# A Fourier mixing block turned over: transposed output, folds on both axes, groups of 384 tokens, the second weight matrix loaded later

## The chip, the cores and the metric

The kernel runs on one core of one Trainium2 chip. The metric is device time in microseconds (us) of one execution; lower is better. The profile names the engines PE (TensorE matmul), PEld (its weight loads), DVE (VectorE), ACT (ScalarE), POOL (GpSimd) and SP (the queue that issues most loads).

## The reference

Two blocks follow each other: attention restricted to equal hash buckets, then a Fourier mixing block with a normalised two-layer network. There are 4 batches, 8 heads, 768 tokens, 64 columns per head, 512 model columns and 2048 hidden ones.

```
q_bits = (q @ proj > 0); k_bits = (k @ proj > 0)       # 6 bits: the bucket
scores = where(q_bucket == k_bucket, q @ k.T / 8, -1e9)
x = softmax(scores) @ v                                # (B, S, H*D) = (4, 768, 512)
mixed = real(fft(fft(x, axis=1), axis=2))              # along tokens, then columns
u = x + mixed
un = (u - mean(u)) / sqrt(var(u) + 1e-6)               # over the 512 columns
out = u + maximum(un @ w_ch1, 0) @ w_ch2
```

The weights arrive as 64-bit floats and all matmuls on the path below run in f32.

## The kernel before, in words

The program is traced in an order written out by hand, and a planner then gives each engine its fixed queue: of the instructions that are ready and whose buffers are free it takes the one that was traced first. Every tile tag has a fixed number of buffers; a tile waits until an earlier one of its tag has had its last use. The main loop (L867) runs attention of batch 0 to 3. Attention is a generator that yields after each half step; at each yield the loop draws steps from a second generator, `other`: in batch 0 one step of `weights`, in batches 1 to 3 two steps of `mix` of the batch before. What is left of `other` at the end of a batch is traced there; the mix of batch 3 comes last, alone.

*Attention* treats heads in pairs, n = 0 to 15. `prepare` (L600) transposes q and k of the pair, makes hash bits on PE and buckets `qb`, `kb`. Then for each half g of the queries (384 each) and each of 6 key tiles c comes a half step, 48 per batch: `weigh` (L660) runs two `sc` matmuls, one per head, on 64 rows of the array each, then `exp` on ACT and two masked products on DVE (L675) into one of three `pk` buffers; DVE adds `pk` to the running sum `acc` (L745); `values` (L681) of the half step before runs two `oo` matmuls, one per head, on 64 columns of the array each. At the last c, `finish` (L694) sums on PE (L702), goes through a chain on DVE (L710 to L721: transpose, reciprocal, broadcast, transpose, product) and transposes the result `xn` back to tokens by columns (L726). `oo` has one of two `ps_o` banks per half.

*Mix* (L759) makes sums and differences of the two token halves (`pm`) and of mirrored columns (`eo`), then `y`, the token transform, on PE (L795, 30 matmuls with 193 columns), mirrors `y` (L804), and for each of three groups of 256 tokens: two times `z`, the column transform (L815, 512 columns), u = x + z, mean and variance, `un`, four transposes (`ut`); 16 times `h` (L841: 4 matmuls with 256 columns, then relu on ACT and DVE in turn); two times `o` (L856, 16 matmuls with 512 columns), u + o and the store (L862). There are 66 mix steps per batch, so at two per half step they are used up after 33 of 48.

*Weights* (L583) load the two weight matrices in 32 pieces. `narrow` (L547) turns each from 64-bit to 32-bit: a load from POOL's queue into `st`, nine DVE instructions on 512 columns, one POOL addition (L581). Its buffer is one of the two of tag `fft`, which the mix uses too.

PSUM has eight banks: two tiles of two banks for `sc` (`ps_sc`), two for `oo` (`ps_o`), two for everything else (`ps_1`, by `pt`, L483). Only the last mix, when `attending` is off, takes tiles of all three in turn. `evac` (L494) copies by DVE and ACT in turn.

Of the kernel before, what the change touches and what calls it, by code (L numbers as in the profile page):

```python
# [10 lines left out]
F32 = mybir.dt.float32  # L11
BF16 = mybir.dt.bfloat16
# [35 lines left out]
def _consts():  # L48
# [24 lines left out]
    for r in range(P):  # L73
        h, bit = divmod(r % 32, NBITS)
        if h < 2:
            pw[r, h] = 2.0**bit
    return {
        "pw": np.ascontiguousarray(pw, dtype=np.float32),
        "seq": np.ascontiguousarray(seq, dtype=np.float32),
# [370 lines left out]
def _main(  # L450
# [73 lines left out]
    pwf = wt([P, 2, P], F32, "fft", "pwf")  # L524
# [10 lines left out]
    NPK = 3  # L535
# [5 lines left out]
    seq = const.tile([P, 2, NT // 2, 2 * NK], F32, tag="seq", name="seq")  # L541
    chan = const.tile([P, NDC, DM], F32, tag="chan", name="chan")
# [3 lines left out]

    def narrow(dst, src, name):  # L547


        st = wt([P, 5 * WC], F32, "fft", name)  # L550
# [32 lines left out]
    def weights():  # L583
        nc.sync.dma_start(seq, cn["seq"].ap())
        nc.sync.dma_start(chan, cn["chan"].ap())
        for wsb, wdr in ((w1, moe_w_ch1), (w2, moe_w_ch2)):
            for c in range(wdr.shape[0] // P):
                for f in range(0, wdr.shape[1], WC):
                    dst = wsb[:, c, f : f + WC]
                    src = wdr[c * P : (c + 1) * P, f : f + WC]  # L590
                    if wdr.dtype == I64:
                        narrow(dst, src, f"st{wdr.shape[0]}_{c}_{f}")
                    else:
                        nc.gpsimd.dma_start(dst, src)
                    yield
# [4 lines left out]
    def prepare(n):  # L600


        ts = {}
        for io, nm in enumerate("qk"):
            tn = nat.pop((nm, n))
            junk = wt([P, S], BF16, "xt", f"sq{nm}{n}")
# [5 lines left out]
            for g in range(2):  # L612
                ps = pt([P, 3, P], f"tr{nm}{n}_{g}")
                for c in range(3):
                    nc.tensor.transpose(
                        ps[:, c, :], tn[:, 3 * g + c].rearrange("p h d -> p (h d)"), ident
                    )
                if nm == "q":
                    dst = tt.rearrange("p (t c) -> p c t", c=NT)[:, 3 * g : 3 * g + 3]
                else:  # L620
                    dst = tt.rearrange("p (c t) -> p c t", c=NT)[:, 3 * g : 3 * g + 3]
                evac(dst, ps)
# [67 lines left out]
    def attention(b):  # L690
        xs[b] = wt([P, NT, DM], F32, "x", f"x{b}")
        pending = []

        def finish():  # L694
# [11 lines left out]
            if g == 0:  # L706
# [13 lines left out]
            xt = wt([P, HALF], F32, "xt", f"xt{n}_{g}")  # L720
            nc.vector.scalar_tensor_tensor(  # L721
                xt, oo[:, 0:HALF], vs, rb, op0=ALU.add, op1=ALU.mult
            )
            ps = pt([P, NT // 2, P], f"xn{n}_{g}")
            for i in range(NT // 2):
                nc.tensor.transpose(ps[:, i, :], xt[:, i * P : (i + 1) * P], ident)  # L726
            t = n % NPAIR
            evac(xs[b][:, 3 * g : 3 * g + 3, t * P : (t + 1) * P], ps)

        for t in range(NPAIR):  # L730
# [5 lines left out]
            for g in range(2):  # L736
                oo = ps_o.tile([P, 512], F32, tag="o", name=f"oo{n}_{g}")
                acc = wt([P, 2, HALF], F32, "acc", f"acc{n}_{g}")
                first = None
                for c in range(NT):  # L740
                    pk = weigh(n, g, c, prep)
                    if c == 0:
                        first = pk
                    else:
                        nc.vector.tensor_tensor(  # L745
                            acc, first[:, :, 0:HALF] if c == 1 else acc,
                            pk[:, :, 0:HALF], op=ALU.add,
                        )
                    if pending:
                        finish()  # L750
                    pending.append((n, g, c, pk, oo, acc, vs))
                    yield
# [4 lines left out]
    out_v = out.rearrange("b (t p) m -> b t p m", p=P)  # L757

    def mix(b):  # L759
# [3 lines left out]
        pm = wt([P, 2, NT // 2, DM], F32, "fft", f"pm{b}")  # L763
        for o in range(2):
            nc.vector.tensor_tensor(
                pm[:, o], x[:, 0 : NT // 2], x[:, NT // 2 : NT],
                op=ALU.subtract if o else ALU.add,
            )

        hd = DM // 2  # L770
        eo = wt([P, NT * (2 * hd + 1)], F32, "fft", f"eo{b}")
        ev = eo[:, 0 : NT * (hd + 1)].rearrange("p (t d) -> p t d", t=NT)
        od = eo[:, NT * (hd + 1) :].rearrange("p (t d) -> p t d", t=NT)
        pf = pm.rearrange("p o t d -> p (o t) d")
        nc.gpsimd.tensor_copy(ev[:, :, 0 : hd + 1 : hd], pf[:, :, 0 : hd + 1 : hd])
        nc.gpsimd.memset(od[:, :, 0:1], 0.0)
        nc.vector.tensor_tensor(
            ev[:, :, 1:hd], pf[:, :, 1:hd], pf[:, :, DM - 1 : hd : -1], op=ALU.add
        )
        nc.vector.tensor_tensor(  # L780
            od[:, :, 1:hd], pf[:, :, 1:hd], pf[:, :, DM - 1 : hd : -1],
            op=ALU.subtract,
        )
        yield


        y = wt([P, NDC, S], F32, "fft", f"y{b}")
        parts = [(ev, 0, P, 0, 0, 1.0), (ev, P, P, 0, 1, 1.0),
                 (od, 0, P, 1, 2, -1.0), (od, P, P, 1, 3, -1.0),
                 (ev, hd, 1, 0, 2, 1.0)]  # L790
        for src, d0, w, tab, ci, sign in parts:
            ps = pt([P, 2, NK], f"y{b}_{ci}_{w}")
            for o in range(2):
                for t in range(NT // 2):
                    nc.tensor.matmul(  # L795
                        ps[0:w, o, :], src[:, o * (NT // 2) + t, d0 : d0 + w],
                        seq[:, tab, t, o * NK : (o + 1) * NK],
                        start=(t == 0), stop=(t == NT // 2 - 1),
                    )
            yr = y[0:w, ci, :]  # L800
            evac(
                yr[:, 0 : 2 * NK].rearrange("p (m o) -> p o m", o=2), ps[0:w]
            )
            nc.vector.tensor_scalar(  # L804
                yr[:, 2 * NK : S], yr[:, S - 2 * NK : 0 : -1], sign, None,
                op0=ALU.mult,
            )
            yield
        for g in range(NT // GTT):
            ut = wt([P, NDC, GT], F32, "ut", f"ut{b}_{g}", 1)  # L810
            for j in range(GTT):
                T = GTT * g + j
                ps = pt([P, DM], f"z{b}_{T}")
                for ci in range(NDC):
                    nc.tensor.matmul(  # L815
                        ps, y[:, ci, T * P : (T + 1) * P], chan[:, ci, :],
                        start=(ci == 0), stop=(ci == NDC - 1),
                    )
                u = x[:, T, :]
                nc.vector.tensor_tensor(u, ps, u, op=ALU.add)  # L820
# [7 lines left out]
                un = wt([P, DM], F32, "un", f"un{b}_{T}", 2)  # L828
                nc.vector.tensor_scalar(  # L829
                    un, u, mv[:, 0:1], rs, op0=ALU.subtract, op1=ALU.mult  # L830
                )
# [103 lines left out]
```

## Time and profile before

| | us |
|---|---|
| median of 3 runs | 1619.61 |
| lowest and highest run | 1619.54, 1631.6 |
| profiled execution | 1626.62 |
| its span, first to last instruction | 1624.8 |
| mean granted TensorE clock | 0.913 |

The page gives busy time per engine, then the span in 40 slices of 40.6 us, each digit a busy share in tenths, and groups of instructions by source line with count, total busy time, mean duration in ns and the idle time of the engine before them. A row of busy time by stage gives the bounds of the stage, its length, each engine's busy time with its count of instructions, and the granted clock. PE is busy also while a matmul only drains, so start-to-start times say more of PE than the mean duration of one matmul.

### The profile page before, as it was taken

The numbers are of one execution on the slowest core, as the hardware profiler recorded it, in microseconds if no ns is written. First come the engines' busy times: TensorE is split into PE (matmuls) and PEld (weight loads), VectorE is DVE, ScalarE is ACT, GpSimd is POOL, SyncE is SP. The second block draws the span as 40 slices with busy tenths as digits, with TensorE's granted clock in tenths as the row PEclk, the third lists the DMA queues.
The fourth block names the chain that finished last, engine by engine and source line by source line (L and its number), as shares of the span: only waits on it lengthen the run. The fifth ranks groups of instructions, "written<-read, shape, count | busy, mean of one in ns | idle before, by whom it ended". The sixth has DMA issues, their size and how long they took to land. (4 is left out here: it accounts for less than half of the span.)

```text
span 1624.8 us, 12841 instructions
## 1 busy us (share of the span) xinstructions
PE 1407.1 (87%) x5074; PEld 717.6 (44%) x5074; DVE 807.0 (50%) x1415; ACT 273.8 (17%) x439; POOL 124.5 (8%) x156
## 2 busy tenths in 40 slices
PE   6556466899999899899998999899998998698987
PEld 2111122256464453355363553455453543565563
DVE  6899999864242435853341427653432528401020
ACT  2101012322020122321120213221120203000000
POOL 2333332000000000000000000000000000000000
PEclk9555577899999899899999899899999999899999
DMA  5222322101000101101000001101001000000000
GB/s 168 85 75 67 94 74 57 29 1 24 19 0 13 30 1 42 30 1 30 13 1 23 20 7 36 29 0 30 13 0 30 13 14 0 0 7 7 7 7 16
DMA packets 82453, 45.23 MB, mean 28 GB/s; under 512 B 76368, under 2 KB 76496, under 8 KB 82128
## 3 DMA queue, kind: packets, MB, share of 16 engines
q1 hardware_dynamic: 75856, 21.25, 5.6%
q0 software_dynamic: 6528, 23.07, 4.2%
q8 instruction: 42, 0.69, 0.2%
q14 instruction: 27, 0.22, 0.1%
HBM read 38.02 MB, written 6.29 MB: 27 GB/s over the span
## 5 line engine op out<-in xcount | busy, mean ns | idle before, releaser
L841 PE MATMUL h<-ut,w 128*128 128x256 f32 x1536 | 354.6, 390 | 2.1 <-ACT ut L500 2.1
L856 PE MATMUL o<-w,hr 128*128 128x512 f32 x768 | 332.2, 593 | 0.0
L841 PEld LDWEIGHTS h<-ut,w 128*128 128x128 f32 x1536 | 294.6, 195 | 65.9 <-issue 23.0
L685 PE MATMUL oo<-pk,vn 128*64 128x385 f32 (+1 forms) x768 | 251.6, 559 | 72.7 <-DVE pk L675 72.7
L675 DVE SCALAR_TENSOR_TENSOR pk<-qb,kb,pk 128x384 f32<-128x384 bf16 x384 | 238.2, 652 | 78.5 <-ACT pk L673 78.3
L673 ACT ACTIVATE pk<-sc 128x768 f32<-128x768 f32 x192 | 155.1, 812 | 650.9 <-PE sc L667 555.8
L667 PE MATMUL sc<-qt,kt 64*128 64x384 f32 x768 | 221.5, 572 | 13.4 <-ACT pk L673 7.8
L856 PEld LDWEIGHTS o<-w,hr 128*128 128x128 f32 x768 | 145.2, 190 | 181.7 <-issue 181.5
L861 DVE TENSOR_TENSOR x<-o,x 128x512 f32<-128x512 f32 x24 | 16.6, 692 | 313.4 <-PE o L856 313.4
L685 PEld LDWEIGHTS oo<-pk,vn 128*64 128x64 f32 x768 | 59.6, 144 | 226.8 <-DVE pk L675 168.3
L847 DVE TENSOR_SCALAR hr<-h 128x256 f32<-128x256 f32 x96 | 40.8, 425 | 236.7 <-PE h L841 236.7
L667 PEld LDWEIGHTS sc<-qt,kt 64*128 64x128 f32 x768 | 76.6, 199 | 132.2 <-issue 81.5
L745 DVE TENSOR_TENSOR acc<-acc,pk 128x768 f32<-128x768 f32 x128 | 122.3, 956 | 3.0
L815 PE MATMUL z<-chan,y 128*128 128x512 f32 x192 | 88.6, 604 | 0.0
L862 POOL DMA_DIRECT2D out_dram<-x x24 | 14.2, 592 | 885.9 <-DVE x L861 786.6
L581 POOL TENSOR_TENSOR w<-st 128x512 f32<-128x512 f32 x32 | 68.8, 2150 | 163.0 <-DVE st L578 163.0
L849 ACT ACTIVATE hr<-h 128x256 f32<-128x256 f32 x96 | 36.9, 385 | 242.6 <-PE h L841 242.6
L795 PE MATMUL y<-seq,eo 128*128 128x193 f32 (+1 forms) x240 | 50.0, 367 | 6.0 <-DVE eo L780 6.0
L815 PEld LDWEIGHTS z<-chan,y 128*128 128x128 f32 x192 | 35.3, 193 | 41.9 <-issue 40.8
L834 PE MATMUL ut<-ident,un 128*128 128x128 f32 x96 | 16.4, 296 | 41.2 <-DVE un L829 41.2
L795 PEld LDWEIGHTS y<-seq,eo 128*128 128x128 f32 (+1 forms) x240 | 40.8, 193 | 17.3 <-issue 7.1
L726 PE MATMUL xn<-ident,xt 128*128 128x128 f32 x96 | 19.8, 320 | 30.5 <-DVE xt L721 30.5
(82 smaller groups left out, 779.2 us busy)
## 6 DMA issues: line engine op xcount, KB each, us to landing
st<-in_moe_w_ch_dram POOLq DMA_DIRECT2D x32, 512.0 KB, 4.0
qn<-in_q_dram SPq DMA_DIRECT2D x32, 192.0 KB, 3.2
kn<-in_k_dram SPq DMA_DIRECT2D x32, 192.0 KB, 3.4
vn<-in_v_dram SPq DMA_DIRECT2D x32, 192.0 KB, 3.3
out_dram<-x POOLq DMA_DIRECT2D x24, 256.0 KB, 2.4
seq<-k_seq SPq DMA_DIRECT2D x1, 1158.0 KB, 8.1
chan<-k_chan SPq DMA_DIRECT2D x1, 1024.0 KB, 7.5
pwf<-k_pw SPq DMA_DIRECT2D x1, 128.0 KB, 2.3
```

The costliest lines, as they stand in the source:

```text
L581: nc.gpsimd.tensor_tensor(dst, val, rest, op=ALU.add)
L667: nc.tensor.matmul(ps[:, h, 0:HALF], kt[rows, c * P : (c + 1) * P], qt[rows, qs], start=True, stop=True,)
L673: nc.scalar.activation(pk[:, :, 0:HALF], ps[:, :, 0:HALF], AF.Exp, scale=SCALE)
L675: nc.vector.scalar_tensor_tensor(pk[:, h, 0:HALF], qb[:, h, qs], kb[:, h, c : c + 1], pk[:, h, 0:HALF], op0=ALU.is_equal, op1=ALU.mult,)
L685: nc.tensor.matmul(oo[h * D : (h + 1) * D, 0:w], nat["v", n][:, c, h, :], pk[:, h, 0:w], start=(c == 0), stop=(c == NT - 1),)
L745: nc.vector.tensor_tensor(acc, first[:, :, 0:HALF] if c == 1 else acc, pk[:, :, 0:HALF], op=ALU.add,)
L795: nc.tensor.matmul(ps[0:w, o, :], src[:, o * (NT // 2) + t, d0 : d0 + w], seq[:, tab, t, o * NK : (o + 1) * NK], start=(t == 0), stop=(t = ...
L815: nc.tensor.matmul(ps, y[:, ci, T * P : (T + 1) * P], chan[:, ci, :], start=(ci == 0), stop=(ci == NDC - 1),)
L841: nc.tensor.matmul(ps, w1[:, c, fc * P : (fc + 1) * P], ut[:, c, :], start=(c == 0), stop=(c == NDC - 1),)
L847: nc.vector.tensor_scalar(hr, ps, 0.0, None, op0=ALU.max)
L849: nc.scalar.activation(hr, ps, AF.Relu)
L856: nc.tensor.matmul(ps, hs[fc][:, j * P : (j + 1) * P], w2[:, fc, :], start=(fc == 0), stop=(fc == NFC - 1),)
```

## The change

The mix works on transposed data. Attention no longer transposes its result back: L721 writes straight into `x`, now 128 columns of a head pair by tokens. The mix folds in both directions before any matmul: head pairs p and p+2 (columns d and d+256) and the two token halves, so `z` holds 8 tiles of 384. The column transform `cs` writes even and odd frequencies into every second PSUM column (24 matmuls with 256 columns per batch); ACT copies the result to `F`, DVE copies it mirrored. The token transform runs 48 matmuls with 193 or 192 columns into two banks, A and B, whose sums and differences DVE adds to `x` four times per column tile, with mirrored reading. So u comes out transposed, as `h` wants it, and the transposes `ut` go. The mean is taken off w1 instead of u (one product with a matrix of 1/512 per 512 columns, then four subtractions), and the factor 1/sqrt(var) is applied after `o`, which relu allows. Only for variance and output is u transposed back (`un`). `h` has groups of 384 tokens instead of 256.

An attention step now treats both query halves of one key tile: 24 steps instead of 48, four `pk` buffers, both `ps_o` banks held until the pair's end, and three steps of `other` instead of two (in batch 0 one, as before). `prepare` orders q by even and odd tokens, so a token tile is stored with one or two strided stores. The loads of the two tables go ahead of the loop. `weights` draws w1 alone in batch 0; w2 follows in batch 1, one piece before each of the first 16 mix steps. `narrow` and the mix share the tags `z` and `F`, with one buffer each, and the hidden layer `hall` is a tile of `F`.

```diff
-    NPK = 3
+    NPK = 4
     def narrow(dst, src, name):
-        st = wt([P, 5 * WC], F32, "fft", name)
+        tag[0] ^= 1
+        st = wt([P, 5 * WC], F32, "zF"[tag[0]], name, 1)
...
+                if wsb is w1:
+                    ps = pt([P, WC], f"wm{f}")
+                    for c in range(NDC):
+                        nc.tensor.matmul(ps, mean, w1[:, c, f : f + WC], ...)
+                    for c in range(NDC):
+                        w = w1[:, c, f : f + WC]
+                        nc.vector.tensor_tensor(w, w, ps, op=ALU.subtract)
...
             nc.vector.scalar_tensor_tensor(
-                xt, oo[:, 0:HALF], vs, rb, op0=ALU.add, op1=ALU.mult
+                xs[b][:, n % NPAIR, g * HALF : (g + 1) * HALF], oo[:, 0:HALF], vs, rb,
+                op0=ALU.add, op1=ALU.mult,
             )
-            for i in range(NT // 2):
-                nc.tensor.transpose(ps[:, i, :], xt[:, i * P : (i + 1) * P], ident)
-            evac(xs[b][:, 3 * g : 3 * g + 3, t * P : (t + 1) * P], ps)
...
+            oos = [ps_o.tile(...) for g in range(2)]
+            accs = [wt([P, 2, HALF], F32, "t3", f"acc{n}_{g}", 3) for g in range(2)]
+            for c in range(NT):
+                new = [weigh(n, g, c, prep) for g in range(2)]
...
+                while pending:
+                    finish()
+                for g in range(2):
+                    pending.append((n, g, c, new[g], oos[g], accs[g], vs))
+                yield
...
+        z = wt([P, 2, 2, 2, HALF], F32, "z", f"z{b}", 1)
+        for cp in range(2):
+            for pc in range(2):
+                e = wt([P, S], F32, "t3", f"e{b}_{cp}_{pc}", 3)
+                nc.vector.tensor_tensor(
+                    e, x[:, cp], x[:, cp + 2], op=ALU.subtract if pc else ALU.add)
+                for par in range(2):
+                    nc.vector.tensor_tensor(
+                        z[:, cp, pc, par], e[:, 0:HALF], e[:, HALF:S],
+                        op=ALU.subtract if par else ALU.add)
+                yield
+        F = wt([P, 2, NT // 2, 4 * hd], F32, "F", f"F{b}", 1)
+        for par in range(2):
+            for t in range(NT // 2):
+                ps = pt([P, DM], f"cs{b}_{par}_{t}")
+                for pc in range(2):
+                    for cp in range(2):
+                        nc.tensor.matmul(
+                            ps[:, pc:DM:2], z[:, cp, pc, par, t * P : (t + 1) * P],
+                            ch[:, cp, pc, :], start=(cp == 0), stop=(cp == 1))
+                nc.scalar.copy(f[:, 0:DM], ps)
+                nc.vector.tensor_copy(f[:, DM:]..., ps mirrored)
+                yield
...
+        for j in range(NDC):
+            pa, pb = (pt([P, HALF + 1], f"{nm}{b}_{j}") for nm in "AB")
+            for par in range(2):
+                for k, ps in enumerate((pa, pb)):
+                    for t in range(NT // 2):
+                        nc.tensor.matmul(ps[:, cols], F[:, par, t, at : at + P],
+                                         sq[:, t, k, cols], ...)
+            for i in range(2):
+                for ps, op in ((pa, ALU.add), (pb, ...)):
+                    nc.vector.tensor_tensor(u, u, f, op=op)
+            yield
+        hall = wt([P, NFC, HALF], F32, "F", f"h{b}", 1)
+        for g in range(2):
+            for fc in range(NFC):
+                ps = pt([P, HALF], f"h{b}_{g}_{fc}")
...
+                yield
+            for j in range(GT):
+                ps = pt([P, NDC, P], f"un{b}_{T}")
+                for c in range(NDC):
+                    nc.tensor.transpose(ps[:, c, :], x[:, c, T * P : (T + 1) * P], ident)
+                nc.scalar.copy(u, ps.rearrange("p c n -> p (c n)"))
...
+                for fc in range(NFC):
+                    nc.tensor.matmul(ps, hs[fc][:, j * P : (j + 1) * P], w2[:, fc, :], ...)
+                    if fc % 4 == 3:
+                        yield
+                nc.vector.scalar_tensor_tensor(u, ps, rs, u, op0=ALU.mult, op1=ALU.add)
+                store(b, T, u)
...
+    def both(one, two):
+        for _ in one:
+            next(two, None)
+            yield
+        yield from two
...
-    other, per_step = weights(), 1
+    other, per_step = weights([(w1, moe_w_ch1)]), 1
...
-        other, per_step = mix(b), 2
+        other, per_step = mix(b), 3
+        if b == 0:
+            other = both(weights([(w2, moe_w_ch2)]), other)
```

224 lines of the change are left out of this document (107 added, 117 removed).

## The prediction

> **What bounds the kernel now.** I read the page's busy shares and its 40 slices first, to see which engine carries which stretch.
>
> ```profile
> PE 1407.1 (87%) x5074; PEld 717.6 (44%) x5074; DVE 807.0 (50%) x1415; ACT 273.8 (17%) x439; POOL 124.5 (8%) x156
> PE   6556466899999899899998999899998998698987
> DVE  6899999864242435853341427653432528401020
> PEclk9555577899999899899999899899999999899999
> ```
>
> For the first seven slices DVE is full and PE is half busy at half its clock; from there on PE is full. So there are two bounds, and I cut the span where the batches change (the columns are PE, PEld, DVE, ACT, POOL busy, then clock and DMA).
>
> ```profile
> 0.00:310.00 310.00, 195.17 (x551) 61.00 (x551) 276.20 (x494) 57.84 (x84) 88.64 (x77) 0.70 0.28 81
> 310.00:668.00 358.00, 334.24 (x1268) 174.15 (x1268) 162.38 (x281) 68.22 (x109) 9.15 (x20) 0.96 0.07 18
> 668.00:1026.00 358.00, 335.42 (x1272) 173.01 (x1270) 163.81 (x282) 68.42 (x111) 9.12 (x20) 0.97 0.07 18
> 1384.00:1625.00 241.00, 211.38 (x710) 137.29 (x710) 39.35 (x71) 12.49 (x30) 8.45 (x19) 0.93 0.02 7
> 626.00:668.00 42.00, 39.09 (x166) 13.36 (x166) 36.12 (x62) 16.16 (x22) 0.66 (x2) 1.00 0.16 35
> 0.00:310.00 310.00, 154.19 (x288) 87.57 (x64) 0.70 0.28 81
> ```
>
> Stage 0 (310 us) is attention of batch 0 with the weight conversion, bound by DVE: the last row, the conversion's tile `st` alone (its columns are DVE and POOL), takes 154.2 of DVE's 276.2. Stages 1 to 3 (358 us each) are attention of one batch with the mix of the batch before, bound by PE. The tail (241 us) is the last mix alone. The row 626 to 668 is the end of stage 1: the mix is used up there, and DVE is the fuller engine again.
>
> PE's own timeline in stage 2 shows what PE time consists of.
>
> ```profile
> 728.72 10.53 PE L841 MATMUL h<-ut,w 128*128 128x256 f32 x48
> 739.17 0.91 PE L667 MATMUL sc<-qt,kt 64*128 64x384 f32 x2
> 744.46 0.92 PE L667 MATMUL sc<-qt,kt 64*128 64x384 f32 x4
> 745.30 0.87 PE L685 MATMUL oo<-pk,vn 128*64 128x384 f32 x4
> 746.10 3.72 PE L841 MATMUL h<-ut,w 128*128 128x256 f32 x16
> 749.75 0.92 PE L667 MATMUL sc<-qt,kt 64*128 64x384 f32 x4
> ```
>
> From start to start, 48 `h` passes take 10.45 us: 0.218 each, 0.85 ns a column. (Each f32 matmul of the program shows as two passes.) Four `sc` passes take 0.84, four `oo` 0.80, sixteen `h` 3.65. At 0.85 ns a column, and two 64-row or 64-column passes at a time, these would be 0.653, 0.653 and 3.48, so each change between the three array shapes costs 0.15 to 0.19, 0.50 us per half step of attention.
>
> **The change, part by part.** Durations are of the profiled run (1626.62 us, span 1624.8); the median of the runs shown is 1619.61, 7.0 lower, and I take that off at the end.
>
> ```profile
> L581 POOL TENSOR_TENSOR w<-st 128x512 f32<-128x512 f32 x32 | 68.8, 2150 | 163.0 <-DVE st L578 163.0
> L552 POOL DMA_DIRECT2D st<-in_moe_w_ch_dram x32 | 18.8, 587 | 18.3 <-DVE pw L527 9.3 <-POOL w L581 8.9
> st<-in_moe_w_ch_dram POOLq DMA_DIRECT2D x32, 512.0 KB, 4.0
> L820 DVE TENSOR_TENSOR x<-z,x 128x512 f32<-128x512 f32 x24 | 16.6, 692 | 43.8 <-PE z L815 43.6
> L498 DVE COPY x<-xn 128x384 f32<-128x384 f32 x16 | 8.8, 551 | 1.6 <-PE xn L726 1.6
> L745 DVE TENSOR_TENSOR acc<-acc,pk 128x768 f32<-128x768 f32 x128 | 122.3, 956 | 3.0
> L675 DVE SCALAR_TENSOR_TENSOR pk<-qb,kb,pk 128x384 f32<-128x384 bf16 x384 | 238.2, 652 | 78.5 <-ACT pk L673 78.3
> L726 PE MATMUL xn<-ident,xt 128*128 128x128 f32 x96 | 19.8, 320 | 30.5 <-DVE xt L721 30.5
> 668.00:1026.00 358.00, 21.90 (x48) 8.64 (x48) 0.97 0.07 18
> 668.00:1026.00 358.00, 12.02 (x60) 9.48 (x60) 0.97 0.07 18
> 626.00:668.00 42.00, 12.19 (x15) 1.00 0.16 35
> 331.76 4.19 PE L795 MATMUL y<-seq,eo 128*128 128x193 f32 x24
> ```
>
> *Stage 0.* Sixteen of the 32 conversions (w2) leave it. One costs DVE 154.2/32 = 4.82: 77 us less. Taking the mean off w1 adds 16 subtractions of 512 columns from PSUM, 0.69 each as at L820: 11 more. Half of eight `xn` evictions of 0.55 go: 2 less. Sum **-68**. The 32 mean passes on PE (0.85 ns x 512 = 0.435 each) and the two tables, which go to SP's queue before the weights instead of with them, lie beside DVE; without that cover the passes would cost 14.
>
> *Stages 1 to 3, PE work.* `z` and `y` cost 21.9 and 12.0 per stage (the two rows with 48 and 60 passes). In their place stand 48 channel passes of 256 columns (0.218: 10.5) and 96 sequence passes of 193 (24 `y` passes took 4.12 to the next row, 0.172: 16.5): **-6.9**. Sixteen `h` groups of 384 columns instead of 256 stream the same columns: 0. The 24 `xn` transposes go: 24 x 0.206 = **-4.9**; the 24 for `un` replace those for `ut`. Both query halves in one step: 24 instead of 48 rounds of three shape changes, 24 x 0.50 = **-12.0**. Three mix steps per attention step spread some 70 mix steps over all 24 instead of ending at half step 33 of 48. The 42 us after 626 hold 15 half steps (the row with x15, of L673, one `exp` each), whose PE work (1.31 and two changes, 1.65 each) with an estimated 10 for one preparation and the closing sums is 35: **-7**, the best case; the worst is 0.
>
> *What it adds there.* Both halves now hold both `o` banks until the end of a head pair, and the second half's closing chain follows the first's on DVE.
>
> ```profile
> 1379.00 0.87 PE L702 MATMUL sum<-acc,ones 128*64 128x384 f32 x4
> 1379.91 0.58 DVE L710 STREAM_TRANSPOSE rt<-sum 128x384 f32<-128x384 f32 x1 [0.97 <-PE sum L702]
> 1382.68 0.55 PE L726 MATMUL xn<-ident,xt 128*128 128x128 f32 x3 [2.82 <-DVE xt L721]
> 1389.21 12.96 PE L795 MATMUL y<-seq,eo 128*128 128x193 f32 x60 [5.99 <-DVE eo L780]
> 1415.32 29.58 PE h L841 x128
> 1444.90 27.47 PE o L856 x64
> 1587.11 27.48 PE o L856 x64
> L498 DVE COPY kt<-trk 128x384 f32<-128x384 f32 x16 | 8.9, 554 | 7.5 <-PE trk L615 7.4
> L498 DVE COPY y<-y 128x386 f32<-128x386 f32 x8 | 4.5, 562 | 3.4 <-PE y L795 3.1
> L498 DVE COPY qt<-trq 128x384 f32<-128x384 f32 x16 | 13.4, 839 | 15.3 <-PE trq L615 15.3
> L500 ACT COPY kt<-trk 128x384 f32<-128x384 f32 x16 | 7.7, 479 | 24.8 <-PE trk L615 24.8
> L500 ACT COPY qt<-trq 128x384 f32<-128x384 f32 x16 | 13.6, 848 | 63.0 <-PE trq L615 63.0
> ```
>
> From the sums to the end of one chain are 3.7 us (1379.00 to 1382.68), of two 6.4, and DVE has one step's four products and two sums (4 x 0.65 + 2 x 0.96 = 4.5) in front: 10.9 per pair if PE stands still, 0 if mix passes fill it. A quarter of the mix, some 50 us of PE, falls to each pair, so I take 1: **+4** per stage. Per stage -6.9 - 4.9 - 12.0 - 7 + 4 = -26.8; three stages **-80**. DVE does more of the mix's folding (four adds of 768 columns and eight of 384 instead of `pm` and `eo`), but has about 195 us free per stage, so this costs nothing unless it is late. ACT, busy 68 of 358, gets six copies of 512 columns more, POOL eight stores more in all (0.59 each): nothing. The sequence passes hold both `ps_1` banks until DVE's four adds (0.56 each, from `kt`'s 554 ns above), so each of the four groups per batch can stop PE for 2.2; attention passes cover that, and without them it is 9 per stage.
>
> *w2 in stage 1.* Its 16 conversions bring DVE 77 us, which has room on average but not at the start, where three per attention step are due. And they use the mix's own single buffers `z` and `F` in turn; the hidden layer `hall` has `F` too, and is written later in the program than all of them. One conversion takes 0.59 + 4.0 + 4.82 + 2.15 = 11.6 us in its buffer. I expect about five of the eight in `F` to come after the transform has freed it: 58 us in which no relu can write, so PE gets no `h` beyond two banks. In that time the two buffers pass ten conversions, 48 of the 58 us of DVE, leaving it two attention steps, some 6 us of PE (2 x (2 x 1.31 + 0.50)). So **+50**. The ends are 0 (conversions run ahead in idle DVE time) and 77 (as serial as they were in stage 0). What waits behind: on POOL the statistics' square root stands behind a conversion's load that waits for its buffer, harmless, since `rs` is used only after an `o` tile's 13.7 us.
>
> *Strided output.* The channel passes write every second PSUM column; no matmul in this trace does. The nearest rows are evictions: stride 8 bytes (`y`, 562 for 386) costs nothing against contiguous (`kt`, 554), stride 24 bytes (`qt`) 1.5 times on DVE and 1.8 on ACT. The stride is the first one's, so I take 0; the other end is doubled, 192 x 0.218 = 42 over four batches. The Trainium skill speaks against my value: "PSUM — Partial Sum Buffer", section Specifications (TRN2), says that PSUM lines are 8 bytes and that any non-contiguous access pattern slows matmuls significantly, without a factor; taken as a doubling, it gives the sum with 42 added.
>
> *Tail.* Before, from the last sums (1379.00) to the last `o` pass (1587.11 + 27.48) are 235.6. After: 6.4 for sums and chains, 4.2 for the folds that need the last pair (2 x 0.96, 4 x 0.56), 10.5 + 16.5, 2.2 for the last adds, 256 `h` passes of 0.327 = 83.6 (now 90.6 with three cold starts), 24 transposes 4.1, `o` unchanged at 3 x 27.5 = 82.4; 210, and 2 for changes: **-24**.
>
> Sum: -68 - 80 + 50 - 24 = -122; 1626.6 - 122 - 7 = **1498**.
>
> **The rivals.** (a) w2 is hidden: stage 1 costs what 2 and 3 do; DVE's 195 us speak for it, the shared buffer against. 1498 - 50 = 1448. (b) w2 costs its full 77: 1525. For it: stage 0, where conversions were never hidden, and its clock of 0.70 where PE waits much. (c) Strided output doubles: 1540. (d) The change doesn't do what it says: the planned order breaks the groups of eight passes up, and the shape changes stay, 3 x 12: 1534. That `h` stands in groups of 48 and of 16 passes between `sc` groups shows an order filled by readiness. (e) Slower: the pair end. If the full 10.9 is paid at all 16 pairs, that is 174 in place of my 12: 1660. Without this term the change gains 134, so it decides from 8.4 us per pair (no gain) and 9.4 (1% slower). For it: PE's order is fixed beforehand, and nothing of another pair's `oo` can fill; against it: mix passes can, in three batches of four.
>
> **How the numbers follow.** Forecast 0.48, (a) 0.16, (b) 0.12, (c) 0.07, (d) 0.07, (e) 0.10, half of it within 1% and half beyond. A measurement here tells about 1% from no change. So faster 0.90, same 0.05, slower 0.05. Range 1440 to 1560: it takes in (a) to (d) and leaves out (e) and mixtures at both ends.
>
> **What would show it.** Stage 0 near 242 us with DVE still about nine tenths busy; `sc` and `oo` in groups of eight passes; stages 2 and 3 near 331 each; stage 1 near 380, with a stretch where PE idles and `h` waits for conversions in `F`; channel passes near 0.218; the tail near 217. It is wrong if stage 1 is as short as stage 2 (a), if channel passes exceed 0.3 (c), or if PE waits over 8 us at each pair's end (e).

## The result, and the profile after

| | before | after |
|---|---|---|
| median, us (4 runs each) | 1620.38 | 1431.87 |
| lowest and highest | 1619.54, 1631.6 | 1428.16, 1434.62 |
| profiled execution, its span | 1626.62, 1624.8 | 1432.43, 1430.6 |

The change is faster: 0.8821 of the time before, 95% interval 0.8777 to 0.8865. That is 66 us below the forecast of 1498 and 8 below the range.

The page of the changed kernel, busy shares and slices (35.8 us each):

```profile
PE 1270.0 (89%) x4642; PEld 618.0 (43%) x4642; DVE 791.5 (55%) x1429; ACT 269.6 (19%) x433; POOL 142.9 (10%) x174
PE   6685677770799999989999999999999999899996
DVE  6988989889743445485544463665434453511010
PEclk9787979995899999999999999999999999999999
```

DVE, full for the first seven slices before, is now at eight or nine tenths from the second slice to the tenth. PE is nearly full only from the twelfth slice on, and in the tenth it has a zero and a clock of half: a hole that the kernel before didn't have. To set the stages side by side I cut both kernels where the last `sum` passes of each batch start. The busy time by stage, first before, then after:

```profile
0.00:311.30 311.30, 196.04 (x555) 61.20 (x555) 277.41 (x495) 57.84 (x84) 88.64 (x77) 0.70 0.27 81
311.30:669.00 357.70, 334.27 (x1268) 174.14 (x1268) 162.14 (x280) 68.61 (x110) 9.15 (x20) 0.96 0.07 18
669.00:1026.00 357.00, 334.53 (x1268) 172.82 (x1268) 162.85 (x281) 68.03 (x109) 9.12 (x20) 0.97 0.07 18
1026.00:1379.00 353.00, 329.51 (x1269) 171.59 (x1269) 162.00 (x281) 66.85 (x106) 9.12 (x20) 0.98 0.06 15
1379.00:1624.80 245.80, 212.79 (x717) 137.80 (x717) 42.59 (x78) 12.49 (x30) 8.45 (x19) 0.94 0.02 7
```

```profile
0.00:227.50 227.50, 161.46 (x560) 54.52 (x560) 193.57 (x360) 55.93 (x85) 65.48 (x47) 0.85 0.27 74
227.50:608.90 381.40, 312.13 (x1157) 153.32 (x1158) 242.47 (x433) 66.94 (x108) 44.25 (x55) 0.91 0.13 37
608.90:912.90 304.00, 299.60 (x1154) 148.42 (x1152) 157.79 (x281) 66.71 (x108) 11.46 (x24) 1.00 0.09 21
912.90:1217.30 304.40, 299.64 (x1156) 148.44 (x1154) 158.00 (x282) 65.10 (x104) 11.47 (x24) 1.00 0.07 17
1217.30:1430.60 213.30, 197.16 (x624) 113.32 (x620) 39.65 (x77) 14.88 (x28) 10.21 (x24) 0.98 0.03 9
```

| stage | before | after | difference | as predicted |
|---|---|---|---|---|
| 0 | 311.3 | 227.5 | -83.8 | -68 |
| 1 | 357.7 | 381.4 | +23.7 | +23 (-27 and +50) |
| 2 | 357.0 | 304.0 | -53.0 | -27 |
| 3 | 353.0 | 304.4 | -48.6 | -27 |
| tail | 245.8 | 213.3 | -32.5 | -24 |
| sum | 1624.8 | 1430.6 | -194.2 | -122 (each -27 is 26.8) |

In stages 2 and 3 PE is now busy for 299.6 of 304 us at full clock: next to nothing is left there but its own passes. PE's idle time in stage 2 fell from 22.5 us (357.0 less 334.53) to 4.4. What it waited for before (total, times, longest):

```profile
PE ut L834 <- DVE un L829: 9.7, 6, 3.4
PE xn L726 <- DVE xt L721: 3.8, 4, 2.8
PE oo L685 <- DVE pk L675: 2.8, 6, 0.7
PE kb L648 <- ACT qb L500: 2.7, 4, 0.7
```

After, in the same view of stage 2, the two longest entries:

```profile
PE trq L647 <- ACT qt L515: 1.1, 1, 1.1
PE cs L830 <- DVE z L817: 1.0, 1, 1.0
```

The waits for `un` and `xt` are gone with their transposes, and nothing at a pair's end took their place. Stage 1 looks right, +23.7 against +23, but only because two errors cancel: by stage 2 the mix and attention saved 53 there, not 27, so w2 cost 77.4 (381.4 less 304.0), not 50. The hole is in PE's timeline, and POOL's shows the conversions inside it:

```profile
312.19 0.86 PE L721 MATMUL oo<-pk,vn 128*64 128x384 f32 x2
365.40 6.78 PE L881 MATMUL h<-x,w 128*128 128x384 f32 x15 [52.34 <-ACT h L890]
...
330.23 1.43 POOL L601 TENSOR_TENSOR w<-st 128x512 f32<-128x512 f32 x1 [3.10 <-DVE st L598]
335.83 1.36 POOL L601 TENSOR_TENSOR w<-st 128x512 f32<-128x512 f32 x1 [3.31 <-DVE st L598]
...
363.46 1.36 POOL L601 TENSOR_TENSOR w<-st 128x512 f32<-128x512 f32 x1 [3.32 <-DVE st L598]
```

The relu (`ACT h`) can't write until the last conversion has left `F`; it does so at 364.8, and PE goes on at 365.4. From 330 on a part is finished every 5.5 us, two buffers in turn.

Three other signs that the prediction named, from PE's timeline in stages 2 and 3:

```profile
629.81 5.45 PE L830 MATMUL cs<-ch,z 128*128 128x256 f32 x24
635.19 1.56 PE L703 MATMUL sc<-qt,kt 64*128 64x384 f32 x8
...
1007.23 1.56 PE L703 MATMUL sc<-qt,kt 64*128 64x384 f32 x8
1008.72 1.51 PE L721 MATMUL oo<-pk,vn 128*64 128x385 f32 x8
1010.16 8.01 PE L881 MATMUL h<-x,w 128*128 128x384 f32 x24
1018.10 1.56 PE L703 MATMUL sc<-qt,kt 64*128 64x384 f32 x8
```

`sc` and `oo` do come in groups of eight, 1.49 and 1.44 us from start to start. A dense step of eight passes at 0.85 ns a column and two at a time is 1.31, so a change of array shape still costs 0.13 to 0.18, but half as often. And 24 channel passes into every second column take 5.38 us (629.81 to 635.19), 0.224 each.

### The profile page after: what moved, and what is told of

It reads as the page before. It is cut to its first block, busy times and chain, and to the rows that moved or that the text cites. A ratio compares the mean times of both kernels' runs of the same rounds, so it can differ in the third digit from the quotient of the medians.

```text
span 1430.6 us, 11986 instructions
## 1 busy us (share of the span) xinstructions
PE 1270.0 (89%) x4642; PEld 618.0 (43%) x4642; DVE 791.5 (55%) x1429; ACT 269.6 (19%) x433; POOL 142.9 (10%) x174
## 4 chain that ended last, share of the span: by engine, by line
PE 69%; DVE 8%; issue 2%; ACT 1%; POOL 1%; DMA 0%; ACTq 0%; DVEq 0%; POOLq 0%
PE o L909 23%; PE h L881 23%; PE sc L703 7%; PE oo L721 6%; PE cs L830 2%; PE B L856 2%; PE A L856 2%; DVE pk L711 1%; PE sum L738 1%; PE bits L664 1%; DVE acc L776 1%; DVE st L583 1%; PE un L897 1%; PE trk L647 1%; PE trq L647 1%
## 5 line engine op out<-in xcount | busy, mean ns | idle before, releaser
L881 PE MATMUL h<-x,w 128*128 128x384 f32 x1024 | 343.5, 492 | 52.8 <-ACT h L890 52.3
L909 PE MATMUL o<-w,h 128*128 128x512 f32 x768 | 343.5, 597 | 1.4 <-DVE h L888 1.4
L881 PEld LDWEIGHTS h<-x,w 128*128 128x128 f32 x1024 | 191.9, 191 | 203.0 <-ACT h L890 53.0
L909 PEld LDWEIGHTS o<-w,h 128*128 128x128 f32 x768 | 141.1, 190 | 179.5 <-issue 171.2
L721 PE MATMUL oo<-pk,vn 128*64 128x384 f32 (+1 forms) x768 | 185.5, 517 | 21.7 <-DVE pk L711 16.2
L703 PE MATMUL sc<-qt,kt 64*128 64x384 f32 x768 | 179.1, 532 | 9.8 <-ACT pk L709 8.9
L721 PEld LDWEIGHTS oo<-pk,vn 128*64 128x64 f32 x768 | 55.2, 138 | 127.4 <-issue 58.0
L830 PE MATMUL cs<-ch,z 128*128 128x256 f32 x192 | 50.7, 414 | 9.0 <-DVE z L817 8.8
L830 PEld LDWEIGHTS cs<-ch,z 128*128 128x128 f32 x192 | 37.2, 204 | 26.1 <-DVE z L817 11.8
L856 PE MATMUL A<-sq,F 128*128 128x193 f32 (+1 forms) x192 | 36.9, 329 | 1.2 <-DVE x L872 1.2
L856 PE MATMUL B<-sq,F 128*128 128x193 f32 (+1 forms) x192 | 36.6, 327 | 0.7 <-DVE F L837 0.5
```

The source lines that it names most:

```text
L703: nc.tensor.matmul(ps[:, h, 0:HALF], kt[rows, c * P : (c + 1) * P], qt[rows, qs], start=True, stop=True,)
L721: nc.tensor.matmul(oo[h * D : (h + 1) * D, 0:w], nat["v", n][:, c, h, :], pk[:, h, 0:w], start=(c == 0), stop=(c == NT - 1),)
L830: nc.tensor.matmul(ps[:, pc:DM:2], z[:, cp, pc, par, t * P : (t + 1) * P], ch[:, cp, pc, :], start=(cp == 0), stop=(cp == 1),)
L856: nc.tensor.matmul(ps[:, cols], f, sq[:, t, k, cols], start=(t == 0), stop=(t == NT // 2 - 1),)
L881: nc.tensor.matmul(ps, w1[:, c, fc * P : (fc + 1) * P], x[:, c, g * HALF : (g + 1) * HALF], start=(c == 0), stop=(c == NDC - 1),)
L909: nc.tensor.matmul(ps, hs[fc][:, j * P : (j + 1) * P], w2[:, fc, :], start=(fc == 0), stop=(fc == NFC - 1),)
```

## The experiments

Each kernel ran beside the kernel before on the same chip; those took 1632.51 beside the first four runs, 1620.29 beside the second four, 1630.05 beside e9 to e11, and 1622.62 (median of 7) beside e12 and e13. All but e13 are single executions. The kernel before alone spread from 1619.5 to 1632.8 over all of these, and stage 0 of one kernel can differ by 9 us (e13 below), so a few us there say nothing. Stages 2 and 3 repeat much better: where their work is unchanged they take 304.0 to 305.3 us in all kernels made from the changed one, and those of e12 are within 0.1 us of before. Stages are cut as above:

| kernel | total | stage 0 | 1 | 2 | 3 | tail |
|---|---|---|---|---|---|---|
| before | 1626.62 | 311.3 | 357.7 | 357.0 | 353.0 | 245.8 |
| e1 mix spread | 1599.84 | 310.1 | 347.3 | 346.5 | 348.2 | 245.7 |
| e5 without `xn` | 1581.53 | 305.5 | 343.6 | 343.0 | 343.6 | 243.8 |
| e6 `ut` from u | 1578.88 | 309.6 | 346.1 | 347.3 | 345.6 | 228.4 |
| e7 the three | 1507.21 | 305.0 | 324.4 | 325.5 | 324.4 | 225.9 |
| e12 w2 later | 1608.25 | 236.3 | 414.4 | 356.9 | 352.9 | 245.8 |
| after | 1432.43 | 227.5 | 381.4 | 304.0 | 304.4 | 213.3 |
| e2 one half per step | 1451.35 | 222.5 | 384.4 | 313.7 | 315.1 | 213.8 |
| e3 four mix steps | 1461.11 | 228.6 | 384.6 | 315.4 | 314.5 | 216.2 |
| e4 w2 in batch 0 | 1472.21 | 340.7 | 305.8 | 305.2 | 304.1 | 214.6 |
| e8 w2 in `z` alone | 1419.81 | 231.5 | 360.9 | 304.6 | 305.2 | 215.6 |
| e10 three parts at once | 1400.89 | 241.5 | 334.8 | 305.2 | 304.0 | 213.5 |
| e11 the same, batch 1 | 1385.69 | 226.4 | 334.7 | 305.3 | 304.1 | 213.5 |

*Where the 53 us of a stage come from.* Five kernels take one part each. First, the kernel before with its mix steps spread over all 48 half steps:

```diff
-    other, per_step = weights(), 1
+    other, per_step = weights(), 48
...
-        for _ in attention(b):
-            for _ in range(per_step):
+        for i, _ in enumerate(attention(b)):
+            for _ in range((i + 1) * per_step // 48 - i * per_step // 48):
...
-        other, per_step = mix(b), 2
+        other, per_step = mix(b), 68
```

> The kernel before, with its 66 mix steps spread evenly over the 48 half steps of a batch instead of two per half step until they are used up. Nothing else changes. Theory (the changed kernel won more than forecast per stage because PE had little to do once the mix was used up): stages 1 to 3 shrink from 357 to between 330 and 342 us each, the whole by 45 to 80 us, to about 1545 to 1580. Rival (that time came from the steps that take both query halves): within 10 us of before, 1612 to 1630.

Stages 1 to 3 are 10.4, 10.5 and 4.8 us shorter, in between the two expectations: on average somewhat more than the prediction's 7, less than the theory I then had.

Second, from the other side, the changed kernel with one query half per step again (in stage 2 PE now changes its array shape 175 times, against 117 in the changed kernel and 159 before):

```diff
-                new = [weigh(n, g, c, prep) for g in range(2)]
+                new = []
+                for g in range(2):
+                    new.append(weigh(n, g, c, prep))
...
-                while pending:
-                    finish()
-                for g in range(2):
+                    if len(pending) > 1:
+                        finish()
                     pending.append((n, g, c, new[g], oos[g], accs[g], vs))
-                yield
+                    yield
...
```

> The changed kernel with its attention step taken apart again: one query half per step, 48 steps, three mix steps per two half steps; all else stays. As the prediction had it (0.50 us per round of shape changes): 12 us more in each of stages 1 to 3, about 1468 in all. Theory (most of the rest came from filling): the same, 1455 to 1480. Rival (both halves per step carries the extra gain as well): 25 to 30 us more per stage, 1505 to 1525.

It loses 9.7 and 10.7 us in stages 2 and 3: the prediction's 12.0 for the shape changes stands, a little smaller. In stage 2 PE is busy for 310.2 us instead of 299.6, 0.18 for each of the 58 changes more.

Third, the changed kernel with its mix drawn faster, to end early as it did before:

```diff
-        other, per_step = mix(b), 3
+        other, per_step = mix(b), 4
```

> The changed kernel with four mix steps per attention step instead of three, so that the mix is used up after 18 of 24 steps, as it was after 33 of 48 before. Theory (attention without mix beside it is slow): 15 to 25 us more in each of stages 2 and 3, 1460 to 1490 in all. Rival: no change beyond 10 us, 1425 to 1442.

Stages 2 and 3 lose 11.4 and 10.1, less than the theory's 15 to 25. Together with e1: a mix that is used up too early costs 5 to 11 us a stage in either design. Not all of this lies at attention's end, though: in stage 2 of e1 the wait for `un` falls too, from 9.7 us to 4.5.

Fourth, the kernel before without the transposes of attention's result (the result stays turned, so the mixing works on other data):

```diff
-            xt = wt([P, HALF], F32, "xt", f"xt{n}_{g}")
+            t = n % NPAIR
             nc.vector.scalar_tensor_tensor(
-                xt, oo[:, 0:HALF], vs, rb, op0=ALU.add, op1=ALU.mult
+                xs[b][:, 3 * g : 3 * g + 3, t * P : (t + 1) * P],
+                oo[:, 0:HALF].rearrange("p (i s) -> p i s", i=3), vs,
+                rb.rearrange("p (i s) -> p i s", i=3), op0=ALU.add, op1=ALU.mult
             )
-            ps = pt([P, NT // 2, P], f"xn{n}_{g}")
-            for i in range(NT // 2):
-                nc.tensor.transpose(ps[:, i, :], xt[:, i * P : (i + 1) * P], ident)
-            t = n % NPAIR
-            evac(xs[b][:, 3 * g : 3 * g + 3, t * P : (t + 1) * P], ps)
```

> The kernel before without the transposes of attention's result back to tokens: the closing product of a half writes straight into x, as 128 rows of a head pair, and the mix goes on as if these were tokens. Left out: those 96 transposes and their evictions, so the output is another function. Theory (their wait on PE, 3.8 us per stage, counts as well as their passes): 7 to 10 us less in each of stages 1 to 3, 1590 to 1605 against about 1630 before. Rival (only the 4.9 us of passes that the prediction took off): 1606 to 1615.

14.1, 14.0 and 9.4 us shorter, in two of three stages more than the theory's 7 to 10: the 24 passes that I costed at 4.9 were a third to a half of it. The wait for `xt` (3.8 in stage 2) goes with them. Some 5 us of stage 2 are neither: PE's other waits there are 1.3 us shorter and its other passes take less from start to start, but what causes this isn't separated.

Fifth, the kernel before with the transposes `ut` reading u, so that they no longer wait for mean and variance (this leaves the normalisation of the hidden layer's input out; the statistics are still computed):

```diff
-                    nc.tensor.transpose(ps[:, c, :], un[:, c * P : (c + 1) * P], ident)
+                    nc.tensor.transpose(ps[:, c, :], u[:, c * P : (c + 1) * P], ident)
```

> The kernel before with the transposes in front of the hidden layer reading u instead of the normalised tile, which is still computed; so the hidden layer gets u itself, and PE waits for the sum u only, not for mean, variance, square root and normalisation. Left out: the normalisation of the hidden layer's input. Theory (the changed kernel gained by taking the statistics off PE's path, which the prediction put at nothing; the trace of before shows 9.7 us of PE waiting for them in stage 2): 8 to 12 us less in each of stages 1 to 3 and 10 to 25 in the tail, 1575 to 1595. Rival (PE's waits there are filled by other work when they go): under 10 us in all.

11.6, 9.7 and 7.4 us off stages 1 to 3, and 17.4 off the tail, with as many passes as before. PE's waits in stage 2 of this run show what went: the entry for `un` is gone, 0.9 us for u is left, and the others stand.

```profile
PE xn L726 <- DVE xt L721: 3.8, 4, 2.8
...
PE ut L834 <- DVE x L820: 0.9, 1, 0.9
```

Then the three edits to the kernel before in one:

> The kernel before with the even spread of mix steps, without the transposes of attention's result and with the hidden layer fed from u: the three single edits together. Left out: these transposes and the normalisation of the hidden layer's input. Theory (the three add up, and with 10 us for both halves per step and 8 for the smaller transforms they make the 53 us that stages 2 and 3 gained): stages 1 to 3 at 322 to 332 us each, 1500 to 1530 in all. Rival (they overlap in one idle time of some 20 us): stages at 335 to 340.

Stage 2 falls to 325.5: -31.5, against -34.2 for the three alone (-10.5, -14.0, -9.7), so they overlap little. Add the shape changes from e2 (-10) and the transforms, whose PE time from start to start in stage 2, idle time left out, went from 33.3 us (`z` and `y`) to 28.2 (`cs`, A and B; -5.1), and some 47 of the 53 us are accounted for. The other 6 are not separated.

*Whether the strided output costs something.* The changed kernel with each frequency's parity in its own 256 columns (the frequencies stand in another order, so the mixing adds another function):

```diff
-                            ps[:, pc:DM:2], z[:, cp, pc, par, t * P : (t + 1) * P],
+                            ps[:, pc * hd : (pc + 1) * hd], z[:, cp, pc, par, ...],
```

> The changed kernel, with the 24 channel passes of a stage writing 256 adjacent columns instead of every second one (the frequencies then stand in another order in F, so what the mixing adds is another function of the input; the work is the same). Theory: the strided output costs nothing, 24 passes took 5.38 us (629.81 to 635.19) or 0.224 us each against 0.218 of the dense ones: 1427 to 1437 us in all, the 24 passes 5.2 to 5.4 us. Rival: a price in the copies to F or in the order of the reads, 2 us a stage or more: 1424 us or less.

1433.58 us against 1432.43, and the same 24 passes in PE's timeline take 631.12 to 636.50, 5.38 us as before:

```profile
631.12 5.45 PE L830 MATMUL cs<-ch,z 128*128 128x256 f32 x24
636.50 1.56 PE L703 MATMUL sc<-qt,kt 64*128 64x384 f32 x8
```

Rival (c) is out. The Trainium skill, "PSUM — Partial Sum Buffer", section Specifications (TRN2), says that any non-contiguous pattern slows matmuls significantly; for f32 passes at stride two the trace disagrees, 0.224 us each with and without the stride.

*What w2 costs, and where.* The changed kernel with w2 back in batch 0, two parts per step:

```diff
-    other, per_step = weights([(w1, moe_w_ch1)]), 1
+    other, per_step = weights([(w1, moe_w_ch1), (w2, moe_w_ch2)]), 2
...
-        if b == 0:
-            other = both(weights([(w2, moe_w_ch2)]), other)
```

> The changed kernel with w2 loaded in batch 0 again, beside w1 (two pieces per attention step). Theory (in stage 1 w2 blocks the buffer of the hidden layer, in stage 0 it takes DVE time, and the two prices are alike): stage 0 rises from 228 to 300 to 315 us, stage 1 falls from 381 to about 304, the whole stays at 1425 to 1445. Rival (moving w2 is a main part of the gain): 1460 or more. Other rival (the move costs more than it brings): 1400 or less.

Stage 1 falls to the length of the others, 305.8, so nearly all of the 77 us of its excess are w2's. But stage 0 pays 113; at two parts a step PE waits there, among other things, for parts of w1 before the mean can be taken (40.9 us in all, 9.1 in the changed kernel). So this is no clean undoing. The theory of 1425 to 1445 missed.

The kernel before with w2 in batch 1 asks the same without that side effect:

```diff
...
-    other, per_step = weights(), 1
+    other, per_step = weights([(w1, moe_w_ch1)]), 1
...
+        if b == 0:
+            other = both(weights([(w2, moe_w_ch2)]), other)
```

> The kernel before, with w2's sixteen parts drawn in batch 1, one before each of the first sixteen mix steps, as in the changed kernel (nothing else changed; w1 keeps its mean). The prediction took 77 us off stage 0 for w2 (16 x 4.82 of VectorE's work) and 84 went in all, though 11 us of subtractions came in. Theory: w2's parts cost stage 0 more than their VectorE work, since TensorE then runs at a lower granted clock: stage 0 falls from 311 to 205 to 225 us. Rival: they cost just that work, and the rest of the 84 comes from attention's own changes (both query halves per step, no xn): stage 0 230 to 240 us. In stage 1 both expect 40 to 80 us more than the 358 of before.

Stage 0 is 236.3, the rival's 230 to 240: w2's parts cost there little more than their VectorE work. Fifteen of them are gone from it; of the 75.0 us that it loses, 70.0 are DVE's time in the tile `st` (154.2 to 84.2). Its row by stage, to be read beside the two first rows above:

```profile
0.00:236.30 236.30, 169.11 (x553) 54.67 (x553) 202.41 (x360) 57.66 (x84) 44.70 (x47) 0.80 0.27 73
```

DVE is busy for 277.41, 202.41 and 193.57 us of 311.3, 236.3 and 227.5: in all three it idles for 33.9. In these three executions the length of stage 0 goes by DVE's work. Stage 1 of e12 takes 56.7 us more than before, so in the kernel before the move gains some 18 us.

Then the changed kernel with w2's conversions in `z` alone, so that `F` is free for the hidden layer:

```diff
+    only_z = [False]
...
-        st = wt([P, 5 * WC], F32, "zF"[tag[0]], name, 1)
+        st = wt([P, 5 * WC], F32, "z" if only_z[0] else "zF"[tag[0]], name, 1)
...
+            only_z[0] = True
             other = both(weights([(w2, moe_w_ch2)]), other)
```

> The changed kernel with all 16 conversions of w2 in buffer z, none in F, the hidden layer's. Theory (stage 1 is long because the hidden layer waits for conversions in F): PE's wait of 52 us for the first relu is gone, and the last conversion, some 11 us each in one buffer, comes about 220 us into the stage, so that the first output tile waits instead: stage 1 at 345 to 365 us against 381, 1396 to 1416 in all. Rival (the 77 us of DVE time that the conversions take make stage 1 long, whatever the buffer): stage 1 stays within 8 us of 381.

The 52 us wait is gone and stage 1 is 20.5 shorter. That shows the shared buffer as the cause of the wait. But now one buffer passes one part in some 11 us, and `o` is late next. The waits of PE and DVE in stage 1 of this run:

```profile
PE o L910 <- POOL w L602: 16.6, 4, 7.1
PE o L910 <- DVE h L889: 7.5, 2, 7.2
...
DVE st L578 <- DMA st<-in_moe_w_ch_dram: 36.0, 14, 5.4
```

DVE stands for 36 us in front of loads that start only when the buffer is free. So the last version reads three parts at a time into `z`, after the mix has left it (ten steps on), with the temporaries in their own 6 KB; in e10 the first three parts go to batch 0:

```diff
+    def late(cs):
+        for i in range(0, len(cs), 3):
+            st = wt([P, 6 * WC], F32, "z", f"raw{cs[i]}", 1)
+            raws = []
+            for k, c in enumerate(cs[i : i + 3]):
+                raw = st[:, 2 * k * WC : 2 * (k + 1) * WC].bitcast(I32)
+                nc.gpsimd.dma_start(raw.bitcast(I64), moe_w_ch2[c * P : (c + 1) * P, :])
+                raws.append(raw)
+            yield
+            for k, c in enumerate(cs[i : i + 3]):
+                tmp = wt([P, 3 * WC], F32, "tmp", f"tmp{c}", 1)
+                convert(w2[:, c, :], raws[k], tmp...)
+                yield
...
     def both(one, two):
+        for _ in range(10):
+            next(two)
+            yield
```

> The changed kernel, with w2's parts read three at a time into z once the mixing has left it, the temporaries in a buffer of their own, and the first three parts read and converted in batch 0's last four steps, which have no weights left. Theory: what stage 1 still pays with the parts in z alone (360.9 us against 304 to 305 of stages 2 and 3) is waits for the transfers, one part in 10.8 us: o for w2 24.6 us, VectorE for the parts 36.0 us. Both go: stage 1 310 to 335 us, stage 0 228 to 242, 1375 to 1405 in all. Rival: the conversions' own work on VectorE is the price, which no order of the transfers takes away: stage 1 345 us or more, 1410 or more in all.

> As the run before, but all sixteen parts in batch 1, none in batch 0. Theory: three parts fewer in stage 0 (0 to 12 us less there), three more to be converted before o can end in stage 1 (8 to 20 us more there): 1380 to 1410 us in all. Rival: VectorE in stage 0 is so full that the three parts cost more there than in stage 1: then this run is the faster by 3 us or more.

Stage 1 is 334.8 and 334.7, at the upper edge of what was expected, with thirteen conversions and with sixteen: three more cost it nothing, where 8 to 20 us were expected. In e11 PE waits 6.9 us at most for a part (7.5 in all), and DVE for no load:

```profile
PE o L927 <- POOL w L605: 7.5, 2, 6.9
```

Even so stage 1 of e11 is 29.4 us longer than its stage 2: PE is busy for 11.5 us more (312.40 against 300.92) and idle for 17.9 more. That part of w2's price is left, and isn't explained.

Between e10 and e11 stage 0 differs by 15 us, which looked like the rival's case. But the profile of e13, the same kernel as e11, has 235.1 there against 226.4, with no more work on DVE (the first row is e11's, the second e13's):

```profile
0.00:226.40 226.40, 160.84 (x560) 53.72 (x560) 193.95 (x360) 55.71 (x85) 64.75 (x46) 0.86 0.27 72
0.00:235.10 235.10, 166.60 (x560) 55.73 (x560) 192.02 (x360) 56.03 (x85) 68.07 (x46) 0.82 0.26 69
```

So two executions of one kernel differ by 9 us in stage 0, at another clock; DVE idles for 43.1 us in the longer one and for 32.5 in the other, so stage 0 doesn't go by DVE's work alone, and what else sets it isn't known. Which place is better for the three parts stays open. e13 was timed four times:

> The changed kernel with w2's sixteen parts read three at a time into z in batch 1, the temporaries in a buffer of their own, measured again in rounds beside the kernel before: 1380 to 1392 us, 0.853 to 0.860 of the kernel before, 40 to 50 us below the changed kernel. If the single look was a lucky one: 1395 or more.

1387.48 us median of 4 (1382.23 to 1393.87), 0.8528 of the kernel before, interval 0.8484 to 0.8572: 44 us below the changed kernel, and the fastest version here. The two were not timed side by side; their ratios to the kernel before, 0.8528 and 0.8821, agree with the difference.

## Why the prediction was wrong

The sign and the order of the terms were right; the sum was 72 us of span too small (-122 against -194.2). By its own steps:

- *"Stages 1 to 3, PE work", transforms -6.9 and shape changes -12.0*: right in mechanism and nearly in size (-5.1 by the timeline, -10 by e2).
- *"The 24 for `un` replace those for `ut`", costed at nothing*: the failed step, in kind. It counted passes. But the passes of `ut` stood behind a chain on DVE (sums, variance, `un`) with PE idle in front of them, and those of `un` wait for nothing that is late. The row was in the trace of before (9.7 us in stage 2, six times), and e6 measures -7 to -12 per stage. In the tail, where the prediction had no term for these waits either, it measures -17.
- *"24 x 0.206 = -4.9" for `xn`*: the same error in part. Groups of three transposes waited for the end of a chain (four times in stage 2, 3.8 us); e5 measures -9 to -14, of which some 5 us are neither passes nor that wait.
- *-7 for spreading and +4 for the pair end*: e1 gives -5 to -10, part of it in the wait for `un`, and no wait at a pair's end shows in stage 2 after, where the longest of all is 1.1 us. So the +4 was nothing, and rival (e) falls with it; that fits mix passes filling the pair's end.
- *"w2 in stage 1", +50*: the mechanism was right as told, down to the place (`hall` behind conversions in `F`, 52.3 us for the predicted 58), and e8 shows it by removing the buffer. The size was off: 77.4. Beside the 52.3 stand 12.6 us of other idle time (69.3 of 381.4 in stage 1, 4.4 in stage 2) and 12.5 more busy time for the same passes (312.13 against 299.60) at a clock of 0.91. The prediction let two attention steps run in the hole. None did: PE stood before the waiting `h` in its fixed order (0.06 us busy), and all 83 instructions of DVE there are conversions (49.3 of 52.4 us). Rivals (a) and (b), 0 and 77: (b) had the size, but by luck, since it meant DVE's work for the conversions, and the 77.4 are made of other things.
- *Stage 0, -68*: the term for w2 was right (77 predicted; e12 gives 75.0 with 15 of the 16 parts gone from the stretch, about 80 for all). The 11 for the mean is 9.9 in the rows of the subtractions. What was missing is some 14 us less of other work on DVE: without the tile `st` (154.2 us before, 74.6 after) and the subtractions, 123.2 before and 109.1 after, of which the term for `xn` had 2. The rows show where most of it went (the first is of before, the second of after):

```profile
L675 DVE SCALAR_TENSOR_TENSOR pk<-qb,kb,pk 128x384 f32<-128x384 bf16 x96 | 72.2, 767 | 4.3 <-ACT pk L673 4.2
L711 DVE SCALAR_TENSOR_TENSOR pk<-qb,kb,pk 128x384 f32<-128x384 bf16 x96 | 62.2, 675 | 0.8 <-ACT pk L709 0.8
```

The same 96 masked products run 10.0 us faster with half of the conversions gone. Of the 64 that stand alone in the timeline of before, 47 have no addition of POOL beside them and take 0.61 us on average; 17 overlap one and take 1.38. So a conversion seems to delay other work of DVE besides its own nine instructions, through its addition on POOL, and the prediction had no term for that. No run isolates it, and as stage 0 of one kernel varies by 9 us, this account isn't exact.

- *Strided output 0*: right (e9).
- *Tail, -24*: measured -32.5. Chains and folds were put at 10.6 us between the last sums and the channel passes. They cost 4.5: ten of the 48 channel passes started at once, and only the rest waited.

```profile
1217.28 0.81 PE L738 MATMUL sum<-acc,ones 128*64 128x384 f32 x4
1218.02 2.79 PE L830 MATMUL cs<-ch,z 128*128 128x256 f32 x10
1224.57 10.23 PE L830 MATMUL cs<-ch,z 128*128 128x256 f32 x38 [3.76 <-DVE z L817]
...
1250.28 10.16 PE L881 MATMUL h<-x,w 128*128 128x384 f32 x31
```

`h` starts 33.0 us after the sums, where the sum had 39.8 (10.6, 27.0 and 2.2): 6.8 of the 8.5.

So of the 26 us that stage 2's sum missed, some 19 (9.7 for `ut`, 9.1 for `xn`) belong to transposes that were priced by their duration alone. For 13.5 of them (9.7 and 3.8) a wait in front that went too is shown; the other 5 belong to `xn` and stay open. Stage 1 agreed to a microsecond by two errors of 26 and 27.

## What to carry to other kernels

When a change removes or moves an operation, look up not only its duration but the idle time in front of it, by its waits in the stage in question; a group of transposes of 0.7 us that stands behind a chain of statistics is worth its wait as well. When late loads share a buffer with something the bounding engine needs, count when the last of them leaves it: that moment can cost more than their work does (52 of the 77 us here), and reading several into one buffer ahead of their use can take more than half of it away (47 of the 77). A stage whose total agrees is no proof of its terms.

## What the hardware showed

How the granted clock follows a hole is seen in the busy time around it in stage 1 of the changed kernel:

```profile
227.50:250.00 22.50, 16.30 (x75) 6.76 (x74) 21.50 (x46) 7.03 (x12) 2.07 (x2) 0.85 0.31 76
250.00:275.00 25.00, 17.30 (x52) 7.84 (x53) 21.76 (x37) 5.74 (x8) 4.88 (x3) 0.90 0.07 21
...
313.00:365.40 52.40, 0.06 (x2) 0.01 (x1) 49.34 (x83) 0.49 (x1) 19.80 (x19) 0.54 0.29 98
365.40:372.20 6.80, 6.80 (x16) 3.90 (x17) 3.76 (x8) 0.49 (x1) 1.26 (x1) 0.75 0.00 0
372.20:380.00 7.80, 7.07 (x45) 2.73 (x45) 4.82 (x12) 2.93 (x6) 0.00 (x0) 1.00 0.47 101
```

In the hole it stands at 0.54, and at 0.75 over the first 6.8 us of work, then at 1.00. The Trainium skill, "TensorE: Matmul & The Clock Gate", Part 1, has the clock at half after an idle window and at full after some 3.4 us of work; 0.75 over twice that time agrees. So the hole itself costs under 2 us beyond its length (6.8 x 0.25 = 1.7, an estimate). In the first 48 us of the stage the clock is 0.85 and 0.90; estimated in the same way from PE's busy time there, that is 2.4 and 1.7 us. The rest of the 12.5 us of longer busy time isn't explained.
